# Early fills on a written pattern, w_in loaded first, state weights on VectorE with factors in PSUM, and a new hand-written order, in an attention-then-PReLU-MLP kernel on one core

## The chip, the cores and the metric

One NeuronCore of a Trainium2 chip runs the whole program. The metric is the device time of one execution in microseconds. The kernel before takes 213.96 us (median of 3 runs, 213.78 to 214.05). Times inside the text are microseconds from the start of one profiled execution, unless marked ns.

## What is computed

The reference runs two attentions between tokens x (8 batches, 8 heads, 512 tokens, depth 64) and a small state (32 rows per head), stacks the results, and puts them through a two-layer MLP with a PReLU.

```python
scores  = scale * x @ state^T            # (B, H, 512, 32)
a       = softmax(scores, -1)
xread   = a @ state                      # tokens read the state
scores2 = scale * state @ x^T            # (B, H, 32, 512)
a2      = softmax(scores2, -1)
sread   = a2 @ x                         # the state reads the tokens
h = rows(concat(xread, sread)) @ w_in    # 4352 x 512 @ 512 x 2048
g = max(h, 0) + alpha * min(h, 0)
out = g @ w_out                          # 2048 x 512
```

Inputs and output are float32; the kernel computes the matmuls in 16 bits with sums in float32.

## The kernel before

**An order written out by hand.** The kernel has no loops over its work at the top. A long string, `ORDER`, lists tokens such as `F.1.9.2`; each token calls one small function, with its numbers as arguments, and the instructions are issued in that order. Every engine runs its own instructions in the order of their tokens and waits at each for its inputs and its buffer. A letter names the engine where there is a choice: `a` ScalarE, `v` VectorE, `p` GpSimd. So moving a token moves it in the queue of its engine only, and an engine whose next instruction waits keeps everything behind it waiting.

**Buffers.** TensorE's results go to eight banks of PSUM: six single ones, named by a last number in a token (`F.1.9.2` writes bank 2), and a pair called "two". A token that names a bank waits until the last reader of the tile that was there has read it.

**Loads.** x of batch 0 comes in two halves of 512 KB over SyncE's queue (line 167), each half in two casts (`cx.j.g`, line 173) to 16 bits. The states of batch 0 come over ScalarE's queue (line 180), and are cast (`stc`, line 237), transposed on TensorE (`stt`) and copied out (`sto`, and `sbd` for a block-diagonal copy, line 249). All else is loaded and cast to 16 bits by GpSimd's queue: the other states (`lst`), x of later batches (`lx`, line 157), w_in in four column blocks (`wi`, line 194) and w_out in four row blocks (`wo`, line 200). In the queue of GpSimd the first load, `wi.0`, stands behind `stc`.

**Attention.** x is transposed on TensorE for batches 0 and 1 (`xt`, copied out by `xo`, line 289) and by DMA later (`xd`). For batch 0 token scores are made in two parts (`tsc`, line 337), later by one matmul set (`sc`, line 299) and a VectorE transpose (`sb`, line 330). The softmax over 32 state rows is: block maxima (`smax`, line 363), the shift (`ssh`, line 368), the exponential on ScalarE (`sexp`), sums and reciprocals `r1` (`ssum`, lines 381 and 382), the weights `an` (`snorm`, line 385), and their transpose `aT` (`wb`, line 393; for batch 0 through TensorE, `at` and `ao`). The softmax over the 512 tokens: `tm`, `nb`, `te`, `tsum`, `tn` (line 436), a DMA transpose `tt`, and the state's reads `rd`, `rdo`.

**MLP.** The state is multiplied with w_in first (`m`, line 484, copied out by `mo`, lines 508 and 510), so that h of 128 features is two matmuls on the weights aT (`F.b.jc.bank`, line 533; for batch 0 the first features are made in halves, `f`). ScalarE makes the negative part (`N`, line 586; `n` for halves), VectorE the PReLU (`G`, line 589; `g` for halves, line 574), both reading the bank. For batches 0 and 1 the second layer is plain: `S.b.q.jc2` (line 603) multiplies two feature blocks with w_out, and `O` copies the rows out. For batches 2 to 7, and for all state rows (called batch 8), it is done by seven half-size products instead of eight (`P`, line 691), which need sums of w_out blocks (`W`, line 646) and of g blocks (`U`, line 670), copies of products (`K`) and final sums (`Q`, line 724), each followed by its output transfer.

**Fills.** `Z.k.n` (line 220) multiplies a zeroed tile by itself n times into bank k; nobody reads the result. There are 51 such matmuls, all before the first feature matmul.

Of the kernel before, what the change touches and what calls it, by code (L numbers as in the profile page):

```python
# [22 lines left out]
f.0.1.0.4 ao.1.a f.0.0.1.2 xt.1.0.0.3 wo.1 mo.2.0.a.1 xo.1.0.1.v mo.1.0.v oma n.0.1.0 g.0.1.0.1 wo.2 n.0.0.1
xo.1.0.0.v m.1.1 mo.1.1.a m.0.1.1.0 f.0.1.1.3 sc.1 mo.0.1.a.0 mo.0.1.a.1 g.0.0.1.0 g.0.0.1.1 mo.2.0.a.0 f.0.0.0.2
n.0.0.0 tsum.0 tn.0.0 F.0.5.1 n.0.1.1 g.0.1.0.0 S.0.2.1.4 N.0.5 tm.1 F.0.7.0 nb.1.a sb.1 g.0.1.1.1 F.0.6.5 te.1.1
te.1.0 g.0.1.1.0 S.0.1.1.3 tn.0.1 g.0.0.0.0 N.0.6 g.0.0.0.1 smax.1 G.0.6 G.0.5 S.0.1.0 m.0.2 mo.0.2.a N.0.7 S.0.2.0
F.0.4.2 F.0.11.5 N.0.4 G.0.7 G.0.4 N.0.11 G.0.11 S.0.0.1.1 lx.2 wo.3 ssh.p.1 tsum.1 W.1.0.p sexp.1 ssum.1 snorm.p.1
# [5 lines left out]
sc.2 tt.1 sb.2 F.1.11.0 tm.2 rdo.0.a smax.2 F.1.13.2 S.0.0.5 mo.2.2.a.1 S.0.0.7 mo.2.2.a.0 N.1.13 G.1.13 N.1.11
O.0.0.a S.0.3.0.5 G.1.11 nb.2.a te.2.1 S.0.3.7 lx.3 S.0.3.2 F.1.15.3 te.2.0 N.1.15 S.0.3.5 G.1.15 F.1.12.1 F.1.6.2
N.1.12 G.1.12 S.0.3.6 N.1.6 S.0.3.3 G.1.6 S.0.2.7 m.3.3.0.3 mo.3.3.v.1 xd.3 ssh.p.2 sexp.2 ssum.2 mo.3.3.a.0 m.3.2
mo.3.2.a F.1.14.1 W.4.0.p S.1.0.6.2 S.0.3.1 N.1.14 G.1.14 F.1.7.0 O.0.2.a N.1.7 G.1.7 S.1.0.4 F.1.3.3 N.1.3 tsum.2
S.0.3.4 S.1.0.0 m.2.3.4.1 O.0.3.a mo.2.3.v.1 mo.2.3.a.0 m.2.1 mo.2.1.a rd.1.0 m.3.0.5.4 mo.3.0.a.0 S.1.0.3 mo.3.0.a.1
S.1.0.5 sc.3 m.4.0.1.5 mo.4.0.a.0 G.1.3 mo.4.0.a.1 W.3.1.p snorm.p.2 wb.2 lx.4 S.1.3.6.3 F.2.3.4 F.2.2.1 F.2.0.5
S.1.0.7 N.2.3 sb.3 tm.3 G.2.3 rdo.1.a smax.3 N.2.2 G.2.2 N.2.0 S.1.0.1 F.2.8.0 S.1.3.7 W.4.1.p tn.2.1 tn.2.0 ssh.p.3
G.2.0 nb.3.a te.3.0 F.2.1.4 N.2.1 S.1.3.1 te.3.1 tsum.3 G.2.1 S.1.0.2 S.1.3.2 tt.2 N.2.8 G.2.8 O.1.0.a F.2.6.1 N.2.6  # L40
G.2.6 S.1.3.0 F.2.14.5 N.2.14 G.2.14 S.1.1.2.4 F.2.9.2 N.2.9 G.2.9 F.2.10.0 N.2.10 G.2.10 rd.2.1 sexp.3 ssum.3 m.3.1
F.2.5.5 mo.3.1.a F.2.11.2 S.1.3.4 S.1.3.3 S.1.2.1.0 S.1.1.3 N.2.11 G.2.11 rdo.2.a U.2.3.0.p N.2.5 xd.4 G.2.5 S.1.2.5
m.4.1.1.2 mo.4.1.a.1 sc.4 tm.4 S.1.3.5 O.1.3.a tn.3.1 F.2.4.5 tn.3.0 F.2.7.2 mo.4.1.a.0 F.2.13.3 N.2.13 lx.5 sb.4
G.2.13 S.1.1.5 tt.3 F.2.12.1 S.1.1.6 S.1.2.7 F.2.15.3 S.1.2.4 smax.4 S.1.2.3 nb.4.a te.4.0 N.2.4 N.2.7 N.2.12 G.2.4
N.2.15 S.1.2.6 S.1.2.2 S.1.1.0 G.2.7 te.4.1 S.1.2.0 O.1.2.a G.2.15 m.4.3 G.2.12 mo.4.3.a m.5.0.5.2 rd.3.3 rdo.3.a
mo.5.0.v.1 xd.5 m.4.2.1.0 mo.4.2.a.0 snorm.p.3 U.2.1.0.p U.2.2.0.p U.2.4.0.p wb.3 S.1.1.1 S.1.1.7 tsum.4 ssh.p.4
S.1.1.4 F.3.9.2 F.3.7.3 mo.5.0.v.0 sexp.4 lx.6 P.2.1.1.1.1 mo.4.2.v.1 N.3.7 O.1.1.a ssum.4 P.2.1.0.0 N.3.9 G.3.7
# [10 lines left out]
N.4.12 G.4.3 P.3.1.1.0 smax.5 F.4.14.4 K.3.1.a N.4.14 G.4.12 U.3.1.0.p U.3.2.0.p P.3.7.0.1.0 U.3.3.0.p G.4.14
P.3.7.1.1 P.3.6.0.0 F.4.15.1 N.4.15 G.4.15 P.3.6.0.1 P.3.6.1.1 N.4.10 G.4.10 P.3.6.1.0 K.3.2.a F.4.8.5 N.4.8 G.4.8
F.4.13.4 N.4.13 G.4.13 P.3.5.1.1 P.3.5.1.0 P.3.5.0.0 m.5.1 mo.5.1.a m.6.2.1.2 mo.6.2.v.0 m.7.3.5.4 mo.7.3.v.0  # L60
P.3.7.1.0 P.3.7.0.0 sc.6 mo.7.3.a.1 mo.6.2.v.1 sb.6 m.6.1.1.5 rd.4.4 mo.6.1.a.0 rdo.4.a m.7.2.2.1 mo.7.2.a.1 U.3.4.0.p
U.4.3.1.p ssh.p.5 U.4.1.0.p U.4.2.0.p smax.6 P.3.5.0.1 P.4.1.1.0.4 K.3.4.a Q.3.1.1 P.3.2.0.0.1 P.4.1.1.1 sexp.5
# [713 lines left out]
```

## Time and profile before

| | us |
|---|---|
| median of 3 runs | 213.96 |
| the profiled execution | 213.49 |
| its span (first to last instruction) | 211.7 |
| end of the last matmul | 207.9 |
| all zero matmuls (line 220), 51 | 8.9 busy, 1.3 waiting ahead |
| state weights on GpSimd (line 385), 128x1024, 7 | 13.3 busy, 1.9 each |

The profile page gives, for each engine, busy time and its share of the span. PE is TensorE, PEld its weight loads, DVE VectorE, ACT ScalarE, POOL GpSimd, SP SyncE. A row of the timeline has the start, the length, engine and line, what is written and read, how many instructions were merged, and in brackets how long the engine stood idle ahead and what released it. The rows of the stretches have, after the length of the stretch, the busy time of TensorE, its weight loads, VectorE, ScalarE and GpSimd with instruction counts, then the granted clock, the share of the DMA engines and the rate in GB/s. Counts of DMA packets are by queue: q0 is what GpSimd issues, q1 what SyncE issues, q10 the state load of ScalarE.

### The profile page before, as it was taken

To read this page: it belongs to the slowest core of one execution; us is meant where nothing else is said; L and a number is where in the kernel's file an instruction comes from. 1 tells how busy PE (TensorE), PEld (TensorE's weight loads), DVE (VectorE), ACT (ScalarE), POOL (GpSimd) and SP (SyncE) were. 2 spreads that over 40 slices of the span, in tenths; PEclk is the share of its full clock that TensorE was granted. 3 is DMA by queue.
4 is the path that set the end of the run, shared out by engine and by line. 5 is a ranking of instruction groups with operands and counts; after the bars stand their busy time and mean duration, and the time that the engine had idled before them with its cause. 6 is when DMAs were issued, how large, how long until landed. Compare 5 with 4: busy or idle time off the path is not lost.

```text
span 211.7 us, 4977 instructions
## 1 busy us (share of the span) xinstructions
PE 202.8 (96%) x1979; PEld 133.1 (63%) x1979; DVE 173.0 (82%) x259; ACT 144.0 (68%) x280; POOL 182.0 (86%) x119
## 2 busy tenths in 40 slices
PE   4999799999999999999999999999999999999992
PEld 2675334444444445675776887666778668888882
DVE  0598999999999999889998788999799898743141
ACT  2678996789999888868977628796836685520100
POOL 2924689939988999999999899999899998999880
PEclk9999999999999999999999999999999999999998
DMA  5999999478998939403270114991141300022224
GB/s 167 159 193 206 207 196 193 88 136 143 174 144 151 170 82 168 82 3 105 60 185 3 50 62 139 116 247 37 54 99 50 104 0 0 3 96 77 89 86 151
DMA packets 52439, 23.68 MB, mean 112 GB/s; under 512 B 38465, under 2 KB 51393, under 8 KB 52417
## 3 DMA queue, kind: packets, MB, share of 16 engines
q0 software_dynamic: 18816, 8.09, 30.8%
q1 hardware_dynamic: 33328, 15.22, 28.8%
q8 instruction: 15, 0.25, 0.5%
q10 hardware_dynamic: 272, 0.07, 0.1%
q14 instruction: 8, 0.06, 0.1%
HBM read 17.31 MB, written 8.91 MB: 124 GB/s over the span
## 4 chain that ended last, share of the span: by engine, by line
PE 90%; DVE 5%; DMA 2%; issue 0%; ACT 0%; POOL 0%; DVEq 0%
PE h L533 25%; PE px L691 21%; PE o L603 13%; PE pv L691 11%; PE py L691 5%; PE m_ps L484 4%; PE h L542 3%; PE z L220 3%; PE sr_ps L457 2%; DMA st<-in_state_dram 2%; DVE g L574 2%; PE sc L299 1%; PE xT_ps L284 1%; PE st_ps L231 1%; DVE g L589 1%; DVE m L508 1%
## 5 line engine op out<-in xcount | busy, mean ns | idle before, releaser
L589 DVE SCALAR_TENSOR_TENSOR g<-neg,oma_sb,h 128x512 f16<-128x512 f32 (+1 forms) x140 | 92.8, 709 | 8.0 <-ACT neg L586 6.1
L586 ACT ACTIVATE neg<-h 128x512 f32<-128x512 f32 (+1 forms) x140 | 74.6, 579 | 24.7 <-PE h L533 14.7
L533 PE MATMUL h<-aT,m 128*128 128x512 f16 x248 | 66.2, 379 | 0.2 <-DVE g L589 0.2
L691 PEld LDWEIGHTS <-gsum 128*128 128x128 f16 x416 | 40.4, 98 | 9.8 <-issue 0.7
L533 PEld LDWEIGHTS <-m 128*128 128x128 f16 x248 | 23.6, 98 | 20.8 <-issue 1.9
L691 PEld LDWEIGHTS <-g 128*128 128x128 f16 x312 | 30.5, 98 | 7.8
L603 PE MATMUL o<-w_out_sb,g 128*128 128x512 f16 x128 | 33.2, 379 | 1.1 <-DVE g L574 1.1
L670 POOL TENSOR_TENSOR gsum<-g,g 128x1024 f16<-128x1024 f16 (+1 forms) x14 | 27.8, 1988 | 1.6 <-DVE g L589 0.8
L670 POOL TENSOR_TENSOR gsum<-gsum,g 128x1024 f16<-128x1024 f16 (+1 forms) x14 | 27.8, 1988 | 0.9
L670 POOL TENSOR_TENSOR gsum<-g 128x1024 f16<-128x1024 f16 (+1 forms) x14 | 27.8, 1990 | 0.3 <-DVE g L589 0.2
L670 POOL TENSOR_TENSOR gsum<-g,gsum 128x1024 f16<-128x1024 f16 (+1 forms) x14 | 27.7, 1990 | 0.3
L691 PE MATMUL px<-ws,gsum 128*128 128x256 f16 x208 | 27.1, 273 | 0.0
L603 PEld LDWEIGHTS <-g 128*128 128x128 f16 x128 | 11.9, 98 | 16.6 <-issue 1.8
L707 ACT COPY kept<-px 128x512 f32<-128x512 f32 (+1 forms) x15 | 8.4, 561 | 20.2 <-PE px L691 20.2
L385 POOL TENSOR_TENSOR an<-ts,r 128x1024 f16<-128x1024 f32 (+1 forms) x9 | 15.4, 1720 | 5.5 <-DVE r L382 4.0
L368 POOL TENSOR_TENSOR ts<-ts,mx 128x1024 f32<-128x1024 f32 x7 | 13.4, 1911 | 6.9 <-DVE mx L363 6.9
L510 ACT CAST m<-m_ps 128x512 f16<-128x512 f32 x28 | 15.6, 596 | 3.3 <-PE m_ps L484 3.1
L724 DVE TENSOR_TENSOR oq<-pv,kept 128x512 f32<-128x512 f32 (+1 forms) x14 | 9.0, 645 | 10.2 <-PE pv L691 5.7
L691 PE MATMUL pv<-ws,gsum 128*128 128x256 f16 x104 | 15.0, 273 | 0.0
L691 PE MATMUL px<-w_out_sb,g 128*128 128x256 f16 x104 | 14.8, 273 | 0.0
L691 PE MATMUL px<-w_out_sb,gsum 128*128 128x256 f16 x104 | 14.5, 273 | 0.0
L691 PE MATMUL py<-w_out_sb,g 128*128 128x256 f16 x104 | 14.5, 273 | 0.0
(75 smaller groups left out, 268.6 us busy)
## 6 DMA issues: line engine op xcount, KB each, us to landing
out_dram<-oq SPq DMA_DIRECT2D x24, 256.0 KB, 2.2
xg<-in_x_dram POOLq DMA_DIRECT2D x7, 512.0 KB, 7.0
w_in_sb<-in_moe_w_in_dram POOLq DMA_DIRECT2D x4, 512.0 KB, 12.3
w_out_sb<-in_moe_w_out_dram POOLq DMA_DIRECT2D x4, 512.0 KB, 12.5
out_dram<-osb SPq DMA_DIRECT2D x8, 256.0 KB, 3.2
x<-in_x_dram SPq DMA_DIRECT2D x2, 512.0 KB, 5.1
out_dram<-oq SPq DMA_DIRECT2D x4, 128.0 KB, 2.1
st<-in_state_dram POOLq DMA_DIRECT2D x1, 224.0 KB, 5.9
```

The costliest lines, as they stand in the source:

```text
L368: engine(e).tensor_tensor(blocks(cols(live["ts", b], j, S)), blocks(scored(b, j)), over_blocks(cols(live["mx", b], j, S // N)), ALU.subtract,)
L385: engine(e).tensor_tensor(blocks(cols(live["an", b], j, S)), blocks(cols(live["ts", b], j, S)), over_blocks(cols(live["r1", b], j, S // N) ...
L484: nc.tensor.matmul(t[N * k : N * (k + 1), :], st_head(b, h)[64 * r : 64 * r + 64, :], w_in_sb[64 * r : 64 * r + 64, c, 512 * f : 512 * (f ...
L510: copier(e)(m_tile(b, f)[:, g, :], t[g])
L533: nc.tensor.matmul(h.rearrange("p (r j s) -> p r j s", r=2, j=2), ms[b, f][:, g, 128 * j : 128 * (j + 1)], weights(b, g), start=(g == 0), ...
L586: nc.scalar.activation(neg, h, RELU, bias=0.0, scale=-1.0)
L589: nc.vector.scalar_tensor_tensor(g_tile(b, jc), negs.pop((b, jc)), oma_sb[:, jc : jc + 1], hs.pop((b, jc)), ALU.mult, ALU.add,)
L603: nc.tensor.matmul(outs[b, q], g_tile(b, jc)[:, 128 * q : 128 * (q + 1)], w_out_sb[:, jc, :], start=not begun and jc == 2 * jc2, stop=left ...
L670: engine(e).tensor_tensor(t, x(), y(), op)
L691: nc.tensor.matmul(pbanks[b, name][:, i, :], of(b, c)[:, j, 128 * i : 128 * (i + 1)], moving[:, 4 * c + j, :], start=not begun and j == 0, ...
L707: copier(e)(t, pbanks[b, "x"])
L724: nc.vector.tensor_tensor(osb, pbanks[b, name], kept[b, add], ALU.add)
```

## The change

- A tile `pattern`, 128x256, is written by GpSimd with an iota ahead of the identity and takes the place of the zeroed tile in the fills. 16 fills are issued ahead of the order; the order has 30 more, the last of them at the very end, ahead of the last copy.
- `wi.0` is the first token. The cast of the first states goes from GpSimd to ScalarE, so that nothing but the constants, the pattern and the identity stands ahead of the loads in GpSimd's queue.
- The state weights of batches 1 to 7 (`snorm`) are multiplied by VectorE; their factors `r1` get a PSUM bank, named in `ssum`. Batch 0 keeps both as they were.
- Six of the 16 token norms (`tn`) run on ScalarE, the rest stay on GpSimd.
- Who copies what is dealt anew: ScalarE has 48 of the 51 `mo` copies (was 40), all 8 `O` (was 7), 16 of 21 `K` (was 15); VectorE has 7 of 8 `xo` (was 4), both `ao` (was 1), 2 of 4 `cx` (was 1).
- All tokens and banks are placed anew. The tokens `W` and `U` carry a `p` in both orders.

The first and last lines of the two orders, and the functions:

```diff
 ORDER = """
-Z.0.9 cx.0.1.a stc stt.0 sbd.0.v Z.1.5 xt.0.0.1.1 cx.0.0.a xt.0.0.0.2 Z.3.6 sto.v cx.1.0.v sbd.1.a xt.0.1.0.3
-xo.0.0.0.v tsc.0.0.4 xo.0.0.1.a cx.1.1.a tsc.0.1 xt.0.1.1.5 smax.0.0 wi.0 xo.0.1.0.a lst ssh.v.0.0 sc.0.0 xo.0.1.1.a
-tsc.1.0.0 Z.1.2 tsc.1.1 sc.0.1 smax.0.1 ssh.v.0.1 lx.1 wi.1 sexp.0.0 wo.0 wi.2 Z.1.5 m.0.0.1.2 tm.0 wi.3 Z.3.11
-mo.0.0.a.1 ssum.0.0 str.1.3 str.0.5 mo.0.0.a.0 Z.4.13 sexp.0.1 ssum.0.1 snorm.p.0.0 at.0.4 sro.1.v xt.1.1.1.0
...
-Q.8.1.1 U.8.4.0.p P.8.3.0.0 P.8.4.0.1 Q.7.0.0 P.8.4.0.0 Q.8.1.0 P.8.3.0.1 Q.8.0.1.a
+wi.0 cx.0.1.a Z.0.3 cx.0.0.v Z.0.3 cx.1.0.v stc.a Z.0.3 stt.0 xt.0.0.1.1 Z.2.3 xt.0.0.0.2 cx.1.1.a xt.0.1.1.3 sbd.1.v
+lst lx.1 wi.1 wo.0 wi.2 xt.0.1.0.4 sbd.0.a xo.0.0.1.v tsc.0.1.5 xo.0.0.0.v tsc.0.0 wi.3 sto.v sc.0.0 xo.0.1.1.a
+xo.0.1.0.v sc.0.1 smax.0.0 ssh.v.0.0 sexp.0.0 tsc.1.0.1 Z.2.3 tm.0 Z.2.3 m.0.0.2.0 Z.3.3 mo.0.0.a.1 ssum.0.0 Z.3.3
+str.0.3 Z.4.3 tsc.1.1 str.1.4 nb.0.a te.0.0 sro.0.a smax.0.1 sro.1.v ssh.v.0.1 snorm.p.0.0 at.0.5 wo.2 ao.0.v
...
+G.0.4 F.0.10.2 N.0.10 m.0.3 G.0.7 mo.0.3.a F.0.11.4 G.0.10 N.0.11 G.0.11 F.0.9.5 m.1.3 N.0.9 G.0.9 F.0.13.3 N.0.13
+tn.0.1.p F.0.8.2 S.0.1.5 F.0.12.4 S.0.3.1.5 S.0.2.5 N.0.8 G.0.13 N.0.12 ssh.p.1 wo.1 sexp.1 F.0.15.3 S.0.3.5 G.0.8
...
+Q.8.1.1 P.8.4.0.1 P.8.4.0.0 Q.8.1.0 U.8.4.1.p P.8.3.0.1 Q.8.0.0 U.8.4.0.p P.8.3.0.0 Z.0.3 Q.8.0.1.a
 """
...
+    pattern = consts.tile([128, 256], F16)
+    nc.gpsimd.iota(
+        pattern, pattern=[[37, 256]], base=-4800, channel_multiplier=29,
+        allow_small_or_imprecise_dtypes=True,
+    )
     ident = consts.tile([128, 128], F16)
     make_identity(nc, ident)
...
-    zero = consts.tile([128, 256], F16)
-    nc.vector.memset(zero, 0.0)
-
-    def zeros(k, n):
-        t = single(k, f"z_{len(zs)}", [128, 256], F32)
+
+    def fill(k, n):
+        t = single(k, f"fill_{len(zs)}", [128, 256], F32)
         zs.append(t)
         for _ in range(n):
-            nc.tensor.matmul(t, zero[:, :128], zero, start=True, stop=True)
+            nc.tensor.matmul(t, pattern[:, :128], pattern, start=True, stop=True)
 
     zs = []
+    fill(0, 16)
...
-    def first_states_cast():
+    def first_states_cast(e):
         live["st0"] = consts.tile([128, 2, D], F16, name="st0")
-        nc.gpsimd.tensor_copy(live["st0"], st0_32)
+        copier(e)(live["st0"], st0_32)
...
-            live["r1", b] = att.tile([128, 2 * S // N], F32, name=f"r1_{b}", tag="r1", bufs=2)
+            if b == 0:
+                live["r1", b] = att.tile([128, 2 * S // N], F32, name=f"r1_{b}", tag="r1", bufs=1)
...
-        if g == 0:
+        if ("tsc", j) not in live:
             live["tsc", j] = single(k, f"tsc_{j}", [128, 2, H, N], F32)
...
-    def state_sum(b, j=None):
+    def state_sum(b, jk):
+        j = None if b else jk
+        if b:
+            live["r1", b] = single(jk, f"r1_{b}", [128, 2 * S // N], F32)
         r1 = cols(live["r1", b], j, S // N)
...
-    def token_norm(b, g):
+    def token_norm(b, g, e):
         e2 = live["e2", b][:, g, :, :]
-        nc.gpsimd.tensor_scalar(
-            e2, e2, live["r2", b][:, g : g + 1], 1.0, ALU.mult, ALU.mult
-        )
+        r2 = live["r2", b][:, g : g + 1]
+        if e == "a":
+            nc.scalar.mul(e2, e2, r2)
+        else:
+            nc.gpsimd.tensor_scalar(e2, e2, r2, 1.0, ALU.mult, ALU.mult)
...
-        "Z": zeros,
+        "Z": fill,
```

More of the change, by code (lines that the diff above doesn't have):

```diff
@@ L23 @@
[L23 to L27, printed above, removed]
@@ L33 @@
[L33 to L37, printed above, removed]
@@ L38 @@
[L38 to L47, printed above, removed]
@@ L58 @@
[L58 to L62, printed above, removed]
@@ new lines @@
+F.0.4.5 F.0.5.4 mo.2.0.a.1 n.0.0.1 nb.1.a n.0.1.1 sb.1 te.1.0 g.0.0.0.0 g.0.1.1.0 te.1.1 S.0.2.1.0 g.0.1.1.1 F.0.6.2
+N.0.6 g.0.0.1.1 g.0.0.1.0 tsum.1 G.0.6 N.0.5 G.0.5 S.0.2.0 S.0.1.1.1 m.0.2 mo.0.2.a F.0.7.3 N.0.7 smax.1 S.0.1.0 N.0.4
+G.0.4 F.0.10.2 N.0.10 m.0.3 G.0.7 mo.0.3.a F.0.11.4 G.0.10 N.0.11 G.0.11 F.0.9.5 m.1.3 N.0.9 G.0.9 F.0.13.3 N.0.13
+tn.0.1.p F.0.8.2 S.0.1.5 F.0.12.4 S.0.3.1.5 S.0.2.5 N.0.8 G.0.13 N.0.12 ssh.p.1 wo.1 sexp.1 F.0.15.3 S.0.3.5 G.0.8
+S.0.2.4 mo.1.3.a G.0.12 ssum.1.2 F.0.14.4 S.0.2.6 S.0.1.6 m.1.2 S.0.3.6 S.0.3.4 snorm.v.1 lx.2 xd.2 wb.1 tn.1.1.a
@@ new lines @@
+S.0.1.4 W.1.1.p S.0.2.2 S.0.1.3 F.1.3.2 tn.0.0.a tt.0 mo.1.2.a N.0.14 S.0.2.3 G.0.14 N.0.15 G.0.15 F.1.10.4 F.1.2.3
+tn.1.0.p N.1.3 G.1.3 N.1.2 G.1.2 S.0.2.7 O.0.2.a tt.1 S.0.3.0 N.1.10 F.1.4.2 N.1.4 G.1.10 G.1.4 S.0.1.7 F.1.9.0
+F.1.11.3 N.1.9 G.1.9 F.1.1.4 N.1.1 G.1.1 S.0.1.2 N.1.11 W.3.0.p G.1.11 S.0.3.2 F.1.6.2 N.1.6 S.0.3.7 O.0.1.a sc.2 tm.2
+m.2.2.0.4 rd.0.3 mo.2.2.a.1 sb.2 mo.2.2.a.0 rdo.0.a F.1.15.1 N.1.15 W.1.0.p G.1.15 nb.2.a S.0.0.5.4 F.1.8.0 N.1.8
+G.1.8 G.1.6 te.2.0 S.0.0.2 S.0.0.1 te.2.1 S.0.0.4 W.2.0.p lx.3 F.1.7.3 smax.2 ssh.p.2 F.1.14.1 F.1.5.0 S.0.0.7 F.1.0.2
@@ new lines @@
+W.4.0.p N.1.14 G.1.14 N.1.7 N.1.5 S.0.3.3 G.1.7 N.1.0 G.1.0 m.3.2 F.1.13.1 mo.3.2.a S.0.0.0 F.1.12.3 S.0.0.3 G.1.5
+xd.3 S.0.0.6 S.1.1.2.2 S.1.0.2.0 N.1.13 G.1.13 N.1.12 tsum.2 sexp.2 O.0.0.a G.1.12 S.1.0.4 S.1.0.0 ssum.2.1 snorm.v.2
+wb.2 O.0.3.a m.2.3.3.4 mo.2.3.a.1 m.2.1 mo.2.1.a S.1.0.3 S.1.1.4 mo.2.3.a.0 tn.2.0.p S.1.1.5 W.2.1.p m.3.3.5.4
+mo.3.3.a.0 sc.3 sb.3 tm.3 rd.1.1 mo.3.3.a.1 m.3.0.3.5 mo.3.0.a.0 S.1.0.5 mo.3.0.a.1 F.2.5.4 N.2.5 F.2.7.3 rdo.1.a
+N.2.7 nb.3.a S.1.1.6 lx.4 F.2.3.5 smax.3 N.2.3 G.2.3 te.3.0 F.2.9.1 G.2.5 S.1.0.1 te.3.1 S.1.0.6 S.1.0.7 O.1.0.a
@@ new lines @@
+N.2.13 S.1.3.6 O.1.3.a tm.4 W.3.1.p S.1.2.6 G.2.13 F.3.2.5 G.2.6 N.2.15 F.3.5.0 N.3.5 W.4.1.p U.2.1.0.p N.3.2 sb.4
+S.1.2.2 F.3.6.3 S.1.2.7 nb.4.a S.1.2.4 N.3.6 G.3.5 te.4.1 G.2.15 G.3.2 lx.6 U.2.2.0.p U.2.4.0.p P.2.1.1.0.1 smax.4
+te.4.0 F.3.11.0 N.3.11 G.3.11 G.3.6 O.1.2.a P.2.1.0.1 P.2.1.0.0 F.3.1.2 N.3.1 G.3.1 F.3.14.5 N.3.14 tsum.4 m.4.3
+m.4.2.4.0 mo.4.2.a.0 mo.4.2.a.1 lx.5 xd.5 G.3.14 P.2.1.1.1 K.2.1.v F.3.4.3 F.3.3.4 N.3.3 F.3.7.2 P.2.2.0.1.0 N.3.4
+G.3.4 U.2.1.1.p P.2.2.1.0 P.2.6.1.0 G.3.3 P.2.2.1.1 N.3.7 G.3.7 U.2.2.1.p P.2.2.0.0 P.2.6.1.1 mo.4.3.a ssh.p.4 sexp.4
@@ new lines @@
+P.2.4.0.0 F.4.5.2 tm.5 F.4.2.5 Q.2.1.0 N.4.9 G.4.9 N.4.5 F.4.7.4 N.4.2 P.2.3.0.0 nb.5.a F.4.4.3 te.5.0 P.2.3.1.0 G.4.5
+G.4.2 N.4.7 N.4.4 U.3.3.1.p U.3.3.0.p F.4.6.0 U.3.1.1.p U.3.2.1.p U.3.1.0.p U.3.2.0.p P.3.1.1.1.2 G.4.7 G.4.4 F.4.0.5
+N.4.6 G.4.6 te.5.1 P.3.1.0.0 N.4.0 P.3.1.0.1 F.4.14.4 N.4.14 sb.5 G.4.0 F.4.13.3 N.4.13 G.4.13 F.4.10.0 N.4.10 G.4.14
+G.4.10 P.2.3.1.1 P.2.3.0.1 Q.2.0.1.a P.3.1.1.0 K.3.1.a F.4.8.5 m.5.1 m.6.2.3.1 N.4.8 mo.6.2.a.0 F.4.12.4 G.4.8
+mo.6.2.a.1 tsum.5 P.3.6.0.0 P.3.6.1.0 mo.5.1.a P.3.6.1.1 m.6.1.0.3 mo.6.1.a.1 N.4.12 m.6.3.1.5 sc.6 smax.5 P.3.6.0.1
@@ new lines @@
+mo.6.1.a.0 P.3.2.1.0.3 K.3.2.a P.3.2.0.1 mo.6.3.a.0 sb.6 smax.6 P.3.7.0.1.0 P.3.2.0.0 G.4.12 U.3.4.0.p ssh.p.5 sexp.5
+mo.6.3.a.1 P.3.5.0.1 P.3.7.1.1 P.3.5.0.0 P.3.5.1.0 P.3.5.1.1 K.3.4.a F.4.11.1 ssum.5.4 snorm.v.5 N.4.11 P.3.7.1.0 lx.7
+U.3.4.1.p P.3.7.0.0 F.4.15.5 N.4.15 F.4.3.4 P.3.2.1.1 Q.3.1.1 P.3.4.0.1 P.3.4.1.0 P.3.3.0.1 P.3.4.1.1 wb.5 G.4.11
+N.4.3 G.4.15 Q.3.0.0 U.4.3.1.p P.3.4.0.0 ssh.p.6 sexp.6 xd.7 G.4.3 F.5.11.1 Q.3.1.0 P.3.3.0.0 N.5.11 G.5.11 U.4.1.1.p
+U.4.2.1.p F.5.5.5 N.5.5 F.5.3.3 P.3.3.1.1 N.5.3 G.5.3 m.7.3.4.0 mo.7.3.a.1 P.3.3.1.0 Q.3.0.1.a mo.7.3.a.0 P.4.1.1.1.1
@@ new lines @@
+N.5.15 G.6.6 tn.5.0.p F.5.4.3 tt.5 N.5.4 P.4.3.0.1 F.5.13.2 N.5.13 U.5.1.0.p U.5.2.0.p G.5.15 G.5.4 G.5.13 P.4.7.1.0
+P.4.3.1.1 Q.4.0.1.a P.4.7.1.1 P.4.7.0.1 m.7.1.5.4 Q.4.1.1 sc.7 sb.7 tm.7 mo.7.1.a.1 m.7.2.3.1 mo.7.2.a.0 mo.7.2.a.1
+P.5.1.0.0.2 U.5.1.1.p mo.7.1.a.0 F.6.3.4 N.6.3 F.6.2.3 N.6.2 G.6.3 F.6.11.1 N.6.11 P.4.4.1.0 P.5.1.1.1 P.4.4.0.0
+F.6.4.5 P.5.1.1.0 F.6.0.4 U.5.2.1.p P.5.1.0.1 N.6.4 nb.7.a G.6.2 te.7.0 N.6.0 G.6.11 P.4.4.0.1 tn.6.1.p tt.6 F.6.15.3
+smax.7 ssh.p.7 K.5.1.a G.6.4 P.4.4.1.1 G.6.0 N.6.15 G.6.15 Q.4.1.0 F.6.5.1 N.6.5 G.6.5 te.7.1 F.6.1.5 N.6.1 tsum.7
```

86 lines of the change are left out of this document (38 added, 48 removed).

## The prediction

> **What bounds the kernel now.** I read the page first, then busy time by stretches, the chain, and the timelines of the first 30 us.
>
> ```profile
> PE 202.8 (96%) x1979; PEld 133.1 (63%) x1979; DVE 173.0 (82%) x259; ACT 144.0 (68%) x280; POOL 182.0 (86%) x119
> PE 90%; DVE 5%; DMA 2%; issue 0%; ACT 0%; POOL 0%; DVEq 0%
> ```
>
> TensorE holds 90% of the chain and GpSimd none of it, although GpSimd is busy 86% of the span: taking work off GpSimd is worth nothing by itself. The stretches show where something else decides.
>
> ```profile
> 15.00:20.00 5.00, 4.83 (x76) 3.45 (x74) 4.39 (x10) 4.42 (x9) 3.37 (x4) 1.00 1.24 206
> 20.00:25.00 5.00, 3.66 (x35) 1.68 (x35) 5.00 (x11) 4.95 (x11) 3.29 (x4) 1.00 1.24 207
> 25.00:30.00 5.00, 4.72 (x34) 1.61 (x33) 5.00 (x9) 4.77 (x9) 3.51 (x2) 1.00 1.28 203
> 30.00:40.00 10.00, 10.00 (x54) 4.39 (x53) 9.59 (x14) 7.65 (x14) 9.07 (x7) 1.00 1.21 179
> ```
>
> The columns after the length are TensorE, its weight loads, VectorE, ScalarE, GpSimd. From 20 to 30 us VectorE has no idle time and TensorE has gaps; from 30 us on TensorE has none. The timelines of VectorE and its neighbours name the anchors:
>
> ```profile
> 5.36 1.14 ACT L173 CAST xg<-x 128x512 f16<-128x512 f32 x2 [2.83 <-DMA x<-in_x_dram]
> 6.61 1.17 POOL L157 DMA_DIRECT2D xg<-in_x_dram  x1
> 6.87 1.16 DVE L173 CAST xg<-x 128x512 f16<-128x512 f32 x1 [0.73 <-DMA x<-in_x_dram]
> 9.84 0.69 DVE L363 TENSOR_REDUCE mx<-tsc 128x16 f32<-128x512 f32 x1 [1.48 <-PE tsc L337]
> 26.33 3.37 DVE L589 SCALAR_TENSOR_TENSOR g<-neg,oma_sb,h 128x512 f16<-128x512 f32 x5
> 28.64 1.04 PE L533 MATMUL h<-aT,m 128*128 128x512 f16 x4
> ```
>
> The first half of x lands at 5.36, the second at 6.87. VectorE's cast of it ends at 8.03; from there its queue runs to the fourth of the five prelus (G.0.4), which ends at 26.33 + 3 x 0.656 + 0.74 = 29.04. F.0.10.2, which reuses that bank, starts at 28.64 + 0.43 = 29.07: VectorE's queue sets this moment, and from it TensorE runs gap-free to 207.9. TensorE's real work ahead of it, at the pace of the rows (0.216 per 512 columns, 0.109 per 256), is 12.9 us. So the time is **when TensorE's queue goes dense, plus work left, plus later stalls**; all the TensorE work but the fills is the same in both orders (the same 376 matmuls of lines 533 and 603, 728 of line 691, and so on).
>
> **The change, part by part.** The time moves by the dense start and by new stalls.
>
> *Fills.* 51 zero matmuls become 16 + 30 on a pattern that GpSimd writes ahead of the identity. iota has no row: bounds are the 128x128 memset (0.20) and a 128x512 tensor op on GpSimd (1.05); I take 0.5, nearest the 128x128 select (0.29) at double size. It puts off GpSimd's first load only. Fills behind stt.0 fall from 42 to 18 (2.0 us less at 0.11 each); the chain below runs through VectorE and has them in its small waits. TensorE's fills take 0.217 each until about 9 us and 0.107 after, though the granted clock reads 1.00 in all these stretches; unbroken fills may bring the faster pace sooner, which shortens transposes by at most 4 x 0.05 each, under VectorE's copies: 0 (price 0.3). The last Z.0.3 (0.33) lies under the last output transfer (3.4 us from the last copy's end at 208.31): 0.
>
> *w_in at once.* GpSimd's cast of the first states moves to ScalarE (0.3 us, behind cx.0.1.a), so GpSimd's seven loads no longer stand behind the 3.54 us wait for the state. wi.0 is issued at about 1.8 instead of 5.09, the rest follow up to 7.6 instead of 10.8. In the transfers' packet counts wi.0's data flowed 2.2 us after its issue began: now at 4.0, and then 1320 of the 2048 packets of x are still to come. What shows sharing:
>
> ```profile
> DMA packets 515, 0.21 MB, mean 262 GB/s; under 512 B 198, under 2 KB 515, under 8 KB 515
> q1 hardware_dynamic: 317, 0.16, 66.9%
> q10 hardware_dynamic: 198, 0.05, 26.8%
> DMA packets 411, 0.21 MB, mean 347 GB/s; under 512 B 4, under 2 KB 411, under 8 KB 411
> q1 hardware_dynamic: 411, 0.21, 114.8%
> ```
>
> The first three lines are 3.2 to 4.0, with the state load (q10) beside x (q1); the last two 4.6 to 5.2, x alone. x moves 396 packets per us beside another queue and 685 alone. Of the delay of x's second half: below, 0 (x came first); at the 396, 1320/396 - 1320/685 = 1.4; at half the engines' time, 1.9; above, one packet of x to one of wi.0 (188 packets per us alone, 9 to 10 us): 512 pairs take 3.5 us, the other 808, paired with lx.1 (719 per us), 2.3, so 5.8 against 1.9: 3.9. I take 1.7, between the nearest row and half, since wi.0's packets are longer than the state's. Behind the waiting cast cx.1.0.v now stand VectorE's sbd.1, both xT copies, sto and everything after; before, sbd and sto went ahead of it. On ScalarE cx.1.1.a waits too, with sbd.0 behind it.
>
> *The casts.* VectorE gets two (was one). The row above took 1.16, ScalarE's 0.62; it ended 0.25 after GpSimd's issue of lx.1 ended (7.78). So 0.3 without an issue beside it, up to 1.16 with one. With x late the second takes 0.4; with x on time (GpSimd issuing to 7.6) it ends near 7.85. The Trainium skill (SBUF — State Buffer, Who interferes with whom) says that a VectorE cast in a two-port mode and a GpSimd instruction exclude each other for a whole instruction; the ending at 7.78 + 0.25 agrees, and by that rule alone both casts would end behind an issue.
>
> *VectorE's startup queue* from the end of that cast to G.0.11, whose bank S.0.1.5 reuses, by start-to-start paces: pairs and stT copies 0.4; 7 xT copies at 0.34, 2.4; maxima and shifts of batch 0, 2.5; two token maxima 2.3; two sums 1.6; sro 1.0; two aT copies 0.7; small ones 0.3; 8 half prelus at 0.40, 3.2; transpose 1.2; smax.1 1.1; 6 prelus at 0.655, 3.9: **20.5**. Before, to G.0.4, the same list gives 18.5 for 21.0 elapsed: waits of 1.48 (for TensorE, behind fills) and 0.46, and 0.6 of small ones. The new order has both large waits covered, as the scores no longer stand behind six fills: 20.5 + 0.7 = 21.2. S.0.1.5 has 14.0 of TensorE work ahead of it, which the kernel before has reached at 29.07 + 1.1 = 30.2. **Shift = cast's end + 21.3 - 30.2 = cast's end - 8.9**: with 6.85 + 1.7 + 0.4 = 8.95 it is +0.05; with x on time (7.85) -1.05; with 3.9 (11.15) +2.25.
>
> *State weights on VectorE.* Seven go from GpSimd (1.91 each, 13.4 in all) to VectorE, at 128x1024 with one operand in PSUM: by its stream transpose 1.24 and its reduction 1.21, 8.7 in all. ScalarE takes over m copies (VectorE: -7 x 0.683 - 1.225), one O and one K (-1.4); VectorE takes 3 xT and 1 aT copies (+1.7) and the cast (+0.7): VectorE +3.7, to 177. ScalarE: +5.2 of m copies, 6 token norms at 0.6, and the swaps: +7.3, to 151. GpSimd: -17.
>
> *Cover.* Between S.0.1.5 and TensorE's 140th us VectorE's queue holds 121.6 us against 127.8 of TensorE: slack 6.2. Before, the like stretch held 118.4 against 129.3: 10.9. VectorE idled 8.4 there (10 less 9.59, 20 less 18.97, and so on to 160 us). If all that idle time stays, 8.4 - 6.2 = 2.2 comes out on TensorE; if it was all TensorE's doing, 0 (a bank held for each r1, from its sum to its weights, is inside this). I take **0.8**, nearer to 0, as the stretch 20 to 30 shows VectorE without any wait when it is late.
>
> *All sums on GpSimd:* lines 646 and 670 have only GpSimd rows already and both orders give every W and U a "p"; it removes nothing, 0. The tail: the last sums U.8.4 wait for products that read their buffers, not for GpSimd, and end about 1 us ahead of their use by their 1.15 each; 0, price 1.
>
> **Sum:** 213.49 + 0.05 + 0.8 = 214.3 for the profiled execution (span 211.7 and 1.8 around it), which lies 0.47 below the median 213.96: **214.8** as a median.
>
> **Rivals.**
> *Faster: x is not delayed.* Its packets were queued first; the row of 396 speaks against, the later start of wi.0 if iota is slow speaks for. -1.05, VectorE with its small waits only: 212.9.
> *VectorE the bound all along:* all of its 8.4 idle us stay, +2.2: 216.2. For it: slack of 6.2 in 128; against: the stretch 20 to 30.
> *x shared packet by packet:* +2.25 + 0.8: 217.0. For it, wi.0's long packets; against, the state load's row, where x kept 317 of 515. The Trainium skill (DMA: Bandwidth & Descriptors, SWDGE vs HWDGE vs iDMA) says that each engine goes round-robin between its queues; no row here shows these two queues under load together, and by that rule the time would be the 217.0 of this rival, the worst for loading w_in early.
> *The change doesn't do what it says:* true of the sums, already priced at 0.
>
> **Chances.** Forecast 0.44 (own range 213.7 to 215.8, a fifth of it within the measurable), x on time 0.32, VectorE bound 0.12, packet by packet 0.12. A change of this kernel below 0.2% (0.43 us) can't be told from none. Faster 0.29, within 0.12, slower 0.59. The range goes from below the faster rival, by its unsure 0.3, to above the slowest: 212.6 to 217.3.
>
> **What would show it.** x's second half landing near 8.5 and VectorE's second cast ending near 9.0; the reduction of line 363 starting 1.4 later with no wait for TensorE; S.0.1.5 near 30; line 385 on VectorE near 1.24 each; VectorE above 97% from 30 to 150 us and small waits of lines 533 and 603 for prelus. Wrong if the cast ends before 8.3, or if TensorE is late for a transfer or a ScalarE copy instead.

## The result and the profile after

The kernel after takes 214.43 us (median of 20 runs, 213.72 to 215.53) and the kernel before, run beside it, 213.81 (213.12 to 214.22): ratio **1.0029, 95% interval 1.0018 to 1.0041**, so 0.6 us slower. The profiled execution spans 212.2 us against 211.7.

From the page, the busy time and the chain by engine:

```profile
PE 203.6 (96%) x1974; PEld 132.5 (62%) x1974; DVE 174.8 (82%) x260; ACT 150.3 (71%) x292; POOL 165.0 (78%) x106
PE 86%; DVE 6%; ACT 4%; DMA 2%; issue 1%; POOL 0%; POOLq 0%; ACTq 0%; DVEq 0%; SPq 0%
```

GpSimd is 17 us lighter, ScalarE 6.3 and VectorE 1.8 heavier, and TensorE's share of the chain fell from 90% to 86%. Busy time by stretches (TensorE, its weight loads, VectorE, ScalarE, GpSimd):

```profile
20.00:25.00 5.00, 4.45 (x30) 1.79 (x28) 4.94 (x10) 5.00 (x13) 0.00 (x0) 1.00 1.24 207
25.00:30.00 5.00, 4.36 (x32) 1.38 (x31) 5.00 (x8) 4.95 (x9) 3.23 (x3) 1.00 0.87 145
30.00:40.00 10.00, 10.00 (x54) 4.36 (x53) 9.07 (x12) 8.28 (x14) 6.05 (x5) 1.00 0.97 129
40.00:60.00 20.00, 19.28 (x216) 8.68 (x215) 19.10 (x25) 17.95 (x36) 13.57 (x9) 1.00 0.81 149
```

Two things differ from before: GpSimd does nothing from 20 to 25 us, and TensorE, which before had no gap from 30 us on, loses 0.7 us between 40 and 60. The timelines of the opening and of S.0.1.5 (line 613):

```profile
1.24 5.28 PE L223 MATMUL fill<-pattern 128*128 128x256 f16 x25 [1.24 <-POOL pattern L184]
6.68 0.43 DVE L173 CAST xg<-x 128x512 f16<-128x512 f32 x1 [1.07 <-DMA x<-in_x_dram]
8.97 0.68 DVE L368 TENSOR_REDUCE mx<-tsc 128x16 f32<-128x512 f32 x1
29.15 0.61 PE L613 MATMUL o<-w_out_sb,g 128*128 128x512 f16 x2
```

The second half of x lands at 6.68 (6.87 before): it isn't late. The first maxima start at 8.97, 0.87 earlier. S.0.1.5 starts at 29.15 where the kernel before had reached the same work at 30.2: the opening won 1.05 us.

Where it went is seen best as **lost time**: the start of a step on TensorE less all TensorE work ahead of it in the order (fills not counted), with the durations of the rows. It grows where TensorE waits, does fills, or takes longer for a step than the rows say: between work 29 and 180 some 2.1 us are of the last kind in every kernel (the kernel before has no gap there), so the rows are to be compared with each other. From the profiled executions:

```
TensorE work ahead   14.0   26.4   29.0   60.0  105.0  180.0    end
before              16.29  16.61  16.68  17.53  18.43  18.84  18.86
after               15.12  15.31  16.33  17.23  18.65  19.01  19.21
```

The kernel after leads by 1.3 us until it has done 26.4 us of work (about 42 us into the span). It loses **1.0 within the next 2.6 us of work**, then grows by 2.68 to work 180 where the kernel before grows by 2.16 (**0.5 more**), and 0.2 at the end. The large step:

```profile
26.77 1.91 POOL L373 TENSOR_TENSOR ts<-ts,mx 128x1024 f32<-128x1024 f32 x1 [7.72 <-DVE mx L368]
29.45 1.16 POOL L157 DMA_DIRECT2D xg<-in_x_dram  x1
37.87 1.73 SPq L280 DMA_TRANSPOSE xT<-xg  x1
39.71 1.39 SPq L452 DMA_TRANSPOSE e2T<-e  x1
43.26 0.41 PE L303 MATMUL sc<-xT,stT 64*32 64x256 f16 x16 [0.52 <-DMA xT<-xg]
44.10 0.68 PE L467 MATMUL sr_ps<-e2T,xg 128*64 128x32 f16 x32 [0.21 <-DMA e2T<-e]
```

GpSimd waits 7.72 us at ssh.p.1 for VectorE's maxima. Behind it in the order stands lx.2, the load of batch 2 (issued at 22.58 before, now at 29.45). The transpose xd.2 on SP's queue waits for that load and goes out at 37.87 (33.95 before), tt.0 behind it on the same queue at 39.71 (36.42), and TensorE waits for both. The chain of waits has the same: `39.71 4.34 DMA e2T<-e`.

### The profile page after: what moved, and what is told of

Same layout as the page of the kernel before. It is cut to its first block, busy times and chain, and to the rows that moved or that the text cites. A ratio compares the mean times of both kernels' runs of the same rounds, so it can differ in the third digit from the quotient of the medians.

```text
span 212.2 us, 4985 instructions
## 1 busy us (share of the span) xinstructions
PE 203.6 (96%) x1974; PEld 132.5 (62%) x1974; DVE 174.8 (82%) x260; ACT 150.3 (71%) x292; POOL 165.0 (78%) x106
## 3 DMA queue, kind: packets, MB, share of 16 engines
q0 software_dynamic: 18816, 8.09, 30.2%
## 4 chain that ended last, share of the span: by engine, by line
PE 86%; DVE 6%; ACT 4%; DMA 2%; issue 1%; POOL 0%; POOLq 0%; ACTq 0%; DVEq 0%; SPq 0%
PE h L543 23%; PE px L701 21%; PE o L613 11%; PE pv L701 10%; PE py L701 5%; PE m_ps L494 4%; PE fill L223 4%; PE h L552 3%; PE sr_ps L467 2%; DMA e2T<-e 2%; DVE mx L368 1%; DVE g L599 1%; ACT m L520 1%; PE sc L303 1%; PE xT_ps L288 1%; ACT neg L596 1%
## 5 line engine op out<-in xcount | busy, mean ns | idle before, releaser
L543 PE MATMUL h<-aT,m 128*128 128x512 f16 x248 | 67.7, 379 | 1.3 <-DVE g L599 0.6
L701 PE MATMUL px<-ws,gsum 128*128 128x256 f16 x208 | 28.0, 273 | 0.0
L520 ACT CAST m<-m_ps 128x512 f16<-128x512 f32 x35 | 19.3, 598 | 3.7 <-PE m_ps L494 3.6
L717 ACT COPY kept<-px 128x512 f32<-128x512 f32 (+1 forms) x16 | 9.0, 566 | 14.1 <-PE px L701 11.0
L701 PE MATMUL pv<-ws,g 128*128 128x256 f16 x104 | 14.3, 273 | 0.0
```

The lines of the kernel that those rows point to most:

```text
L520: copier(e)(m_tile(b, f)[:, g, :], t[g])
L543: nc.tensor.matmul(h.rearrange("p (r j s) -> p r j s", r=2, j=2), ms[b, f][:, g, 128 * j : 128 * (j + 1)], weights(b, g), start=(g == 0), ...
L701: nc.tensor.matmul(pbanks[b, name][:, i, :], of(b, c)[:, j, 128 * i : 128 * (i + 1)], moving[:, 4 * c + j, :], start=not begun and j == 0, ...
L717: copier(e)(t, pbanks[b, "x"])
```

## The experiments

Each row's ratio is against runs of the kernel before on the same chip. "Work" columns are lost time as above, of the profiled execution.

```
                          median  ratio  interval            work 14  work 29  29 to 180
e1  lx.2 early            213.77  1.0011  0.9995 to 1.0026    15.97    16.32     2.66
e2  loads gated again     214.70  1.0044  1.0032 to 1.0056    15.70    17.01     2.66
e3  fills on zeros        214.15  1.0028  1.0016 to 1.0040    15.55    16.59     2.66
e4  weights on GpSimd     235.20  1.1048  1.1002 to 1.1094
e5  e1, 12 lead fills     213.16  0.9994  0.9974 to 1.0015    14.52    14.87     2.66
e6  e1, weights twice     221.01  1.0352  1.0334 to 1.0370    15.69    17.28     8.83
e7  e1, no sums           212.92  0.9974  0.9961 to 0.9987    15.68    16.03     2.28
e8  w_in first of all     215.48  1.0093  1.0074 to 1.0113    16.67    17.67     2.66
e9  e5, alpha late        224.43  1.0519  1.0496 to 1.0542    25.70    26.05     2.65
e10 e9, 9 lead fills      224.23  1.0517  1.0492 to 1.0542    27.26    27.59     2.65
e11 e5, factors in SBUF   221.51  1.0356  1.0314 to 1.0397    16.31    16.73    10.12
e12 e5, ScalarE evicts    214.35  1.0039  1.0026 to 1.0052    15.12    15.47     3.82
```

**e1: lx.2 early.** The only edit:

```diff
-ssh.p.1 wo.1 sexp.1 ... snorm.v.1 lx.2 xd.2
+wo.1 lx.2 ssh.p.1 sexp.1 ... snorm.v.1 xd.2
```

> The changed kernel with wo.1 and lx.2 moved ahead of ssh.p.1 in GpSimd's queue, nothing else. Theory A (the load of batch 2 stands behind a shift that waits 7.7 us for VectorE's maxima, so the DMA transposes come late and TensorE waits 0.52 + 0.21 us at 43 us, with 0.3 more around it): the load is issued near 19 instead of 29.5, both waits go, and the time falls by 0.7 to 1.0, to about 213.5, below the kernel before. Theory B (VectorE, with the state weights, is what TensorE waits for from 30 us on): VectorE is just as late, the waits turn into waits for prelus, less than 0.3 is won.

Timeline of e1:

```profile
20.67 1.16 POOL L157 DMA_DIRECT2D xg<-in_x_dram  x1
27.62 1.92 POOL L373 TENSOR_TENSOR ts<-ts,mx 128x1024 f32<-128x1024 f32 x1 [5.79 <-DVE mx L368]
35.31 1.80 SPq L280 DMA_TRANSPOSE xT<-xg  x1
```

The load is issued ahead of the wait, the transpose goes 2.56 us earlier, and both of TensorE's waits are gone: lost time grows by 0.16 from work 26.4 to 29 in place of 1.02. Theory A is right about the waits. In the trace that is worth 0.86; the medians, by the ratios, show 0.4 with overlapping intervals, and e1 is not below the kernel before. Openings differ from one execution to the next (e1's profiled one starts its first maxima 0.86 later than that of the kernel after, with the same instructions; see e5).

**e2: the loads gated again.** The cast of the first states goes back to GpSimd, ahead of wi.0 (`stc.p wi.0 cx.0.1.a ...`).

> The changed kernel with the cast of the first states back on GpSimd, ahead of wi.0, so that all of GpSimd's loads stand behind the arrival of the state again. If early loading delays the second half of x (the prediction's 1.7), this is faster by that and x lands earlier than 6.67. If x was never delayed and the loads merely come earlier than needed, x lands at 6.67 to 6.85 again and the time is within 0.3 of the changed kernel's. If the early weights are what gives the earlier start (S.0.1.5 at 29.15), it is slower by 0.5 or more, with waits of TensorE for DMA before 25 us.

x's halves were cast at 4.96 and 6.55, within what the profiled runs with the loads at once show (4.83 to 5.20 and 6.33 to 6.70): the early loads cost x nothing. TensorE's wait for lx.1 rose from 0.7 to 1.2 us, and the time is 0.3 us above the kernel after, with overlapping intervals, so that the early loads are worth something is not shown. VectorE's second cast took 1.15 us here, and ended at 7.70, 0.25 behind the end of GpSimd's issue of lx.1 (6.27 to 7.45), as in the kernel before; in the kernel after it took 0.43 although GpSimd was issuing w_in loads (5.90 to 7.41, the cast at 6.68). So in these runs it is the issue of lx that holds a cast up, not that of w_in, and the rule of the Trainium skill (SBUF — State Buffer, Who interferes with whom) that the prediction weighed goes too far if every issue is taken for an instruction of that kind.

**e3: fills on zeros.** A VectorE memset of zeros takes the place of iota.

> The changed kernel with the pattern tile zeroed by VectorE instead of written by iota; as many fills in the same places. Same matmuls, zero data. If what the fills multiply does not matter, the fast pace of matmuls (0.107 instead of 0.217 per 256 columns) begins at the same time and the time is within 0.3. If data that changes is needed for it, the slow pace lasts longer than in the changed kernel and 0.3 to 1 us is lost in the transposes of x and the state.

214.15, in line with the kernel after: what the fills multiply does nothing measurable here.

**e4: the state weights on GpSimd, in the new order.** `snorm.v.1` to `snorm.v.7` become `snorm.p`, the factors go to SBUF, and lx.2 is early.

> As e1_lx2_first, with the state weights of batches 1 to 7 back on GpSimd and their factors in SBUF. Against e1: if VectorE's 8.7 us of weights cost TensorE time (the prediction's 0.8 or more), this is faster than e1 by 0.5 to 1 us. If VectorE has cover, it is not faster, and may be slower by the longer chain (1.91 instead of 1.24 per batch).

TensorE waits 13.1 us for GpSimd's sums of g blocks (lines 697 and 676). In this order the weights stand right behind VectorE's sums in the tokens, so GpSimd's queue comes to them early and stands there, with the sums of g blocks behind. From the groups of instructions of e4 (after the second bar, the idle time ahead and what ended it):

```profile
L389 POOL TENSOR_TENSOR an<-ts,r 128x1024 f16<-128x1024 f32 x7 | 13.4, 1913 | 19.8 <-DVE r L386 19.8
```

In the kernel before the same group has 1.5 us of idle time ahead. The loss against e1, 21 us, is more than these waits: in the stretches from 80 to 100, 130 to 140 and 170 to 180 us the granted clock is 0.83 in place of 1.00. So the weights can't be taken back alone in this order; the old order with the weights on VectorE was not run.

**e5: fewer leading fills.** As e1, with `fill(0, 12)` for `fill(0, 16)`.

> The kernel after with wo.1 and lx.2 ahead of ssh.p.1 (as e1), and 12 leading fills in place of 16. If the leading fills are what holds the first states' transposes (they ended at 6.52 us in the profiled run of the kernel after and at 7.38 in e1, with the cast they wait for done by 6.0), four fewer of 0.217 us move the first maxima up by at most 0.87 us, and by 0.3 to 0.6 in an execution like e1's: the median about 213.3 (e1 was 213.77). Rival: the fills also set how early TensorE's pace doubles, and what is saved at the front is lost again at the slow pace behind it: 213.7 to 214.2, with the first maxima no earlier than 9.0.

The first maxima start at 8.38, and the median is 0.4 us below e1's by the ratios, with overlapping intervals: as fast as the kernel before, not faster. The first maxima are 1.45 us earlier than in e1's profiled execution, but four fills are 0.87 at most: that execution is nearly e1's slowest (214.26), and the one profiled here is the fastest of twelve (212.62, with three at 214.4 to 214.5). The leading fills (these and the nine that follow, all queued ahead of stt.0) hold the start: the cast that stt.0 waits for ends by 6.0 in the kernel after, the fills at 6.52.

**e6: the weights twice, and e7: no sums.** Both as e1. In e6 the multiply of batches 1 to 7 stands in `for _ in range(2 if b else 1):`; in e7 `nc.vector.memset(r1, 1.0 / N)` replaces the reduction and the reciprocal of those batches.

> As e1, and every state-weight multiply of batches 1 to 7 is done twice on VectorE (the same result): 7 more instructions of 1.23 us, 8.6 us more of VectorE, with nothing else touched. If the growth of lost time that the kernel after has over the kernel before between 45 and 105 us (about 0.5 us) is the first 8.6 us that VectorE took over, the second 8.6 us costs as much or more: 0.5 to 3 us over e1's 213.77, and the lost time grows in the steps behind each state_norm. Rival: VectorE's load has cover to spare and the growth comes from the new places: less than 0.3 us over e1.

> As e1, without the row sums and reciprocals of the state softmax of batches 1 to 7 (left out: these batches are scaled by 1/32 in place of their sums): some 10 us less of VectorE, in the same places as the work that the change put there. If VectorE's load costs TensorE time in this order: 0.3 to 0.8 us below e1's 213.77. Rival: its load is covered, and the median stays within 0.2 of e1's.

Both say that VectorE's load costs time. Its busy time from 30 to 150 us, from the stretches, against what TensorE loses from work 29 to 180:

```
            VectorE busy of 120   TensorE busy of 120   lost, 29 to 180
e7                108.5                 120.0                2.28
before            112.2                 120.0                2.16
after             115.3                 119.2                2.68
e1                116.0                 119.9                2.66
e6                116.8                 114.5                8.83
```

112 of 120 costs nothing in the old order (TensorE has no gap there), 116 in e1 costs 0.4 against e7, and of the next 8.6 us of work little can be taken in: against e1 VectorE gets only 0.8 us busier in these 120 and TensorE loses 6.2 more, and a further 1.25 ahead of work 29. The waits of e6 (total, times, longest) name VectorE and the multiply:

```profile
PE h L544 <- DVE an L394: 3.2, 3, 1.3
PE pv L702 <- DVE an L394: 0.9, 1, 0.9
```

**e8: w_in ahead of everything.** `load_w_in(0)` moves above the loads of x0, ahead of iota.

> The kernel after with w_in's first slice issued on GpSimd ahead of everything else, iota and identity included: issued at some 0.9 us in place of 1.65. The prediction's term for x's second half (1.7 us later, between 0 and 3.9) rested on the two queues sharing the engines' packets while x is under way; in the kernel after w_in's data first flowed at 5.5 us, when x was nearly through. If its first data come a fixed time behind the issue (3.9 us), they now flow from 4.8 and x's second cast moves from 6.67 to between 7.0 and 7.8: the median 214.5 to 215.2. Rival: they wait until x's queue thins out, wherever the issue stands, and the second cast stays at 6.7: 214.2 to 214.6.

```profile
1.25 0.96 POOL L178 DMA_DIRECT2D w_in_sb<-in_moe_w_in_dram  x1 [0.81 <-POOLq L772]
2.72 5.34 PE L225 MATMUL fill<-pattern 128*128 128x256 f16 x25 [2.72 <-POOL pattern L193]
6.51 0.43 DVE L173 CAST xg<-x 128x512 f16<-128x512 f32 x1 [1.06 <-DMA x<-in_x_dram]
```

Both expectations are wrong about the time, and the rival is right about x. Issued 0.4 us earlier, w_in still has no packet between 5.2 and 5.6 us while x's queue moves 272, and 30 between 5.6 and 6.0: its data wait until x thins out, and x isn't delayed. What I had overlooked is that the issue puts iota off by 1.48 us, the 25 fills with it, and so the start (first maxima at 10.52). Again the fills hold the opening.

**e9: alpha late.** As e5; alpha's DMA leaves the head of SP's queue and follows a memset of its tile on VectorE behind tm.0.

```diff
+    def load_alpha():
+        nc.vector.memset(alpha_sb, 0.0)
+        nc.sync.dma_start(alpha_sb, moe_alpha.rearrange("(jc p) -> p jc", p=128))
```

> As e5 (12 leading fills, lx.2 early), and alpha's load is issued only behind a small VectorE memset that stands after token_max of batch 0 (at some 11 us in place of 1.9). In the kernel after alpha's 4-byte packets took every second turn of the engines from 7 to 12 us, and TensorE waited 0.7 to 0.9 us for lx.1 at 14 us. If those turns delay the loads on GpSimd's queue, lx.1 lands 1.5 to 2.5 us earlier (13.0 or before, from 14.7), the wait for it goes, and the median falls 0.5 to 0.9 below e5's: 0.995 to 0.9975 of the kernel before. Rival: the turns cost the loads little, because a 4-byte packet is short: lx.1 within 0.5 us of where it was, the median within 0.2 of e5's (ratio 0.9985 to 1.0005), or alpha itself is late for its first reader at 15.5 and costs 0.5.

It failed by 11 us, and showed how the queues share. Packet counts of e9 from 13 to 14 us, with alpha not yet flowing, and from 16 to 17 (q0 is GpSimd's queue, q1 SP's):

```profile
q0 software_dynamic: 201, 0.20, 123.5%
...
q0 software_dynamic: 198, 0.20, 119.8%
q1 hardware_dynamic: 197, 0.00, 27.0%
```

The two queues take turns, one packet for one, 198 to 197. The Trainium skill (DMA: Bandwidth & Descriptors, SWDGE vs HWDGE vs iDMA) has the rule that the prediction weighed, that each engine goes round-robin between its queues, and the trace agrees. But the turns of 4-byte packets cost the loads next to nothing (198 packets per us against 201), and the price falls on alpha: its 2048 packets wait for as many long ones. Issued at 10.96, it had landed by 25.68, and VectorE stood 10.07 us for it at oma. lx.1 was no earlier. In the order as it was, alpha has the head start that it needs.

**e10: nine leading fills, first states first.** As e9, with `fill(0, 9)` and `stc.a` ahead of `cx.0.1.a`.

> As e9, with 9 leading fills in place of 12 and the cast of the first states ahead of x's first cast on ScalarE. If the leading fills are still what holds TensorE's first step (5.93 us in e5), the first states' transposes start 0.6 earlier and the median falls by 0.3 to 0.6 more. Rival: x's second half, cast by 6.9, is the limit now: the first maxima stay within 0.15 us of e9's and the median within 0.15.

The median equals e9's (ratios 1.0517 and 1.0519): nothing is won, as the rival said. The profiled execution is the slowest of e10's five (225.62; the others 224.04 to 224.36) and fits neither expectation: the transposes of the first states start at 6.04, no earlier than e9's 5.92, and the first maxima at 9.61, 1.2 later than e9's 8.38. What differs in it is TensorE's pace. The same 12 transposes in e10 and, below, in e5:

```profile
7.70 1.44 PE L291 MATMUL xT_ps<-ident,xg 128*128 128x128 f16 x12
```

```profile
7.09 0.83 PE L288 MATMUL xT_ps<-ident,xg 128*128 128x128 f16 x12
```

In this execution, with 18 fills ahead, the slow pace reached the real work. It did so in e11 too, with 21, so that the number of fills decides it is not shown.

**e11: the factors in SBUF.** As e5; r1 of batches 1 to 7 comes from the SBUF pool again (two buffers), and nothing else is touched.

> As e5, with the factors of the state softmax (r1) of batches 1 to 7 in SBUF in place of PSUM, and nothing else touched. If the factors' place matters to VectorE or, over GpSimd's reads of SBUF, to GpSimd, the weights' 1.23 us change by more than 0.1 us or GpSimd's 0.55 us adds grow, and the median moves by over 0.4 (e6 showed each extra 1.23 us at this place to cost TensorE about 1 us). Rival: the place is worth nothing: 1.15 to 1.30 us an instruction, median within 0.3 of e5's (ratio 0.998 to 1.001).

The seven multiplies took 17.5 us in place of 8.5. From the groups of instructions of e11 (busy time, mean ns of one), and from its timeline the longest of them with what GpSimd does beside it:

```profile
L390 DVE TENSOR_TENSOR an<-ts,r 128x1024 f16<-128x1024 f32 x7 | 17.5, 2497 | 0.2
```

```profile
115.67 2.14 POOL L677 TENSOR_TENSOR gsum<-g,gsum 128x1024 f16<-128x1024 f16 x1
117.63 5.21 DVE L390 TENSOR_TENSOR an<-ts,r 128x1024 f16<-128x1024 f32 x1
117.77 2.12 POOL L677 TENSOR_TENSOR gsum<-g 128x1024 f16<-128x1024 f16 x1
119.85 1.90 POOL L372 TENSOR_TENSOR ts<-ts,mx 128x1024 f32<-128x1024 f32 x1
```

The multiply is issued while GpSimd is in an add, outlasts that one, the next add and the shift (to 121.75), and ends at 122.84, 1.09 us later, about its own length. The other six took 1.33 to 2.99, and GpSimd pays too: three of its 2.13 us adds, each started while the multiply ran, took 3.1. The same group of instructions in the kernel after:

```profile
L393 DVE TENSOR_TENSOR an<-ts,r 128x1024 f16<-128x1024 f32 x7 | 8.5, 1219 | 0.2
```

The Trainium skill (SBUF — State Buffer, Who interferes with whom) says that a VectorE instruction with two SBUF inputs contends with a GpSimd instruction that reads SBUF, and one with at most one SBUF input, outside its two-port modes, does not; the trace agrees on both sides: with the factors in PSUM all seven take 1.21 to 1.22 us (in e5) beside the same adds. So the factors' place, for which the prediction's sum has no term, is worth 7.7 us here by the ratios, 7.5 of it behind work 29.

**e12: four evictions to ScalarE.** As e5, `mo.4.0.v.0`, `mo.5.3.v.0`, `mo.7.0.v.0` and `K.2.1.v` become `a`.

> As e5 (12 leading fills, lx.2 early), with the four evictions of PSUM that VectorE does between 67 and 98 us (three halves of m and one kept bank, 0.68 us each, 2.7 us in all) given to ScalarE, whose busy share is 71%. If VectorE's load is what the order loses time on (e7: 10 us less of it gave 0.4 us in the profiled run; e6: 8.6 us more cost 7.3), 0.1 to 0.4 us come back: 0.9970 to 0.9990 of the kernel before. Rival: ScalarE has no more cover there than VectorE had (its prelu halves stand ahead of the same steps), and the time is e5's or up to 0.5 us above it: 0.9994 to 1.0020.

Slower than e5 by 0.45%, the rival's direction and more. From the timeline of e12, and from its waits (total, times, longest):

```profile
89.09 1.23 DVE L389 TENSOR_REDUCE r<-ts 128x32 f32<-128x1024 f32 x1 [1.81 <-ACT m L520]
```

```profile
PE h L543 <- DVE an L393: 1.0, 1, 1.0
```

Batch 4's sum writes bank 5, which holds the half of m that VectorE had evicted. ScalarE comes to it only at 89 us, VectorE stands 1.81 us, and TensorE 1.0 behind it: a factor in PSUM waits for whoever empties the bank.

No version beats both kernels: e5 equals the kernel before within its interval, and e7, below it, leaves work out.

## Why the prediction held, and where it did not

**The sign and nearly the size held; the way there did not.** Forecast +0.05 for the opening and +0.8 for VectorE, +0.85 in all; measured 0.6 between the medians. In the profiled executions it is -1.3 by work 26.4, +0.95 from there to 29, +0.5 in the middle and +0.2 at the end: +0.35 of lost time for +0.5 of span. That the total came out near is luck: the -1.3 and the +0.95, neither of them in the sum, nearly cancel. By its own signs the prediction is wrong: the cast ended at 7.11, before 8.3, and TensorE was late for two transfers.

- *x's second half 1.7 us late:* **this step failed.** It took w_in's data to flow a fixed 2.2 us behind the issue. Their first packets came at 5.6, 3.9 behind it, with x nearly through, and at 5.7 in e8 with an earlier issue. So both "packet by packet" on x and the 396 packets per us had no object. What keeps w_in's first packets back so long stays open. The 396 were also an average over a stretch in which the state's queue thins out: from 3.2 to 3.6 x moved 128 packets and the state 122, one for one, which speaks for the rival and not against it.
- *Shift = the cast's end - 8.9:* with x on time the rival gave -1.05, and S.0.1.5 came 1.05 early. That agreement is luck: the cast took 0.43 with w_in's issue beside it and ended at 7.11, not 7.85, and VectorE's queue took 22.0 us from there, not 21.3. The 0.7 is one wait for the second scores, which the prediction held to be covered:

```profile
13.18 0.69 DVE L368 TENSOR_REDUCE mx<-tsc 128x16 f32<-128x512 f32 x1 [0.78 <-PE tsc L342]
```

- *Fills, 0 (price 0.3):* the mis-sized term. Those second scores stand on TensorE behind 15 fills (2.6 us, from 9.47 to 13.02), while the data of the steps between them had landed by 9.55 (w_in) and 10.72 (the states); no run leaves these fills out. The 25 ahead of stt.0 take 5.4 us at the prediction's own 0.217, longer than the states' cast needs (done by 6.0). In e8 they start 1.48 later, and the first maxima 1.55 and the median 1.4 later than in the kernel after. Two slips in the working change nothing in the sum: 24 fills fewer at 0.11 are 2.6 us, not 2.0, and VectorE's list adds up to 20.6, not 20.5.
- *VectorE's cover, 0.8 (0 to 2.2):* right mechanism, and right within what was measured: 0.5 between the kernels in the middle, 0.4 by e7's trace (2.66 - 2.28), 0.8 by its median with some 0.4 either way. The rival "bound all along" overstated the first 3 us and would have been right about the next: e6 pays 7.3 for 8.6.
- *State weights at 1.24 each:* 1.22 measured, only because of the PSUM factors (e11). VectorE in all rose by 1.8, not 3.7; 1.0 of the difference is the casts, two at 0.43.
- *The wait that was not named:* the prediction listed what stands behind VectorE's waiting cast, but not what stands behind GpSimd's ssh.p.1, which in the new order waits 7.72 us for VectorE (1.94 before). lx.2 there, then SP's two transposes, cost 0.86 (e1). I counted SP's queue as untouched.
- *Sums on GpSimd, 0:* right, its sums took the same 2.13 us each. *Tail, 0 (price 1):* 0.2 more there; its cause stays open.
- What won the opening's 1.1 us stays open in part. VectorE's cast of x's second half ended 0.9 earlier, and its wait of 1.48 us for the first scores is gone. e2 (loads gated) and e3 (zeros) reach work 14 with 15.70 and 15.55 lost, between the 15.12 of the kernel after and the 15.97 of e1, which has the same opening: so neither the early loads nor the pattern is shown to matter. The fills behind stt.0 and the first cast's engine were not tried apart.

## What to carry to other kernels

Before moving an operation that waits, list the DMA issues behind it on its queue, and the transposes that wait for those on other queues; a load that needs nothing goes ahead of the waiting instruction. An engine at 96% of a stretch (115 of 120 us here) has no cover left though it holds only 6% of the chain: the next 8.6 us there cost 7.3. Where GpSimd adds nearly all the time, give a two-operand VectorE instruction one operand from PSUM, and check who empties its bank.
